# One plan for another: 2239 steps of a fused retention and SwiGLU kernel in a new order

## The chip, the core and the metric

The kernel runs on one core of one Trainium2 chip. The core has five engines that each work through their own instructions in order and wait for one another by semaphores: PE (TensorE, the matmuls, with PEld for its weight loads), DVE (VectorE), ACT (ScalarE), POOL (GpSimd) and SP (SyncE), which here issues nearly all DMA transfers. The metric is the device time of one launch in microseconds (us). Three runs of the kernel before took 639.87, 640.2 and 643.35 us; the median is 640.2 us.

## What is computed

A recurrent retention block (4 batches, 8 heads, 768 positions, head size 64) feeds a SwiGLU feed-forward block (3072 tokens, model size 512, hidden size 1536), all in float32:

```python
gamma = 1.0 - 2.0 ** (-5.0 - np.arange(H, dtype=np.float32))
for t in range(S):
    state = gamma[None, :, None, None] * state + np.einsum('bhd,bhe->bhde', k[:, :, t], v[:, :, t])
    y[:, :, t] = scale * np.einsum('bhd,bhde->bhe', q[:, :, t], state)
...
x = np.ascontiguousarray(attn_out.transpose(0, 2, 1, 3)).reshape(B * S, H * D)
g = x @ w_gate
silu = g * (1.0 / (1.0 + np.exp(-g)))
val = x @ w_val
return (silu * val @ w_out).astype(np.float32)
```

## The kernel before

**Arithmetic.** Every float32 operand of a large product is split into three parts of fewer bits ("near" for weights and hidden values, "far" for tokens), and a product is three groups of matmuls that add up in one PSUM bank. A split is three small steps on a tile: part 0 on ACT, part 1 on DVE, part 2 on DVE or on POOL. So each product of PE waits for pieces of ACT, DVE and POOL.

**Stages.** The 3072 tokens go in four segments, numbered 0 to 3, of 768 tokens each. A segment has its attention, an up stage (gate and value products, 12 units f of the hidden size) and a down stage (12 units f by 6 token blocks). Segment 0's up stage also converts and prepares the weights, and its down stage writes the split down weights to DRAM for the later ones. Segments 1 to 3 compute the up products by seven half-size products of sums (as in Strassen's method). The attention of segment s + 1 runs among the down stage of segment s.

**Order.** All instructions of the kernel belong to named steps. `run()` goes through one string, `PLAN`, and issues each step's instructions when its name comes up; each engine then executes its own in that order. An engine's order is thus what `PLAN` leaves when all other engines' steps are struck out; SP's and ACT's transfers are ordered in the same way. Semaphores are derived from which buffers the steps read and write.

**Names** (`s/` is the segment; segment 0's up stage has none):
- `G f:i`, `W f:i`: gate and value product of unit f in segment 0, 12 matmuls of 384 columns each (L1056); `p`, `v` the same in pieces of 256 columns (L1074). `i f:i` is the silu on ACT (L462), `j f:i` the multiplication on DVE (L462).
- `n f:0` to `n f:5`: the splits of unit f's gate weights (0, 1, 2) and value weights (3, 4, 5) on ACT, DVE and POOL (L1128, L1131, L1134).
- `U` loads raw weights; `a`, `b`, `c` (ACT; L552, L555, L558), `S` (DVE, L565) and `C` (DVE L573 or POOL L575) convert them; `T` makes sums of them on DVE (L417); `Z` stores them.
- `s/p f.n`: the seven products of unit f in segments 1 to 3, six matmuls each (L1229); `s/u f.n` the ten small steps behind them (L1244 to L1248) on ACT and DVE; `s/w f.g.0` to `.2` the splits of group g of unit f's weights (L1128, L1131, and L417 on DVE or L1134 on POOL); `s/L f` their load from DRAM (L1201).
- `s/D f.tok`: three matmuls of 512 columns of the down stage (L1298); `s/h f.k` the splits of the hidden values; `s/W f` the load of the down weights (L1277); `0/d f.0` to `.2` their splits in segment 0 (L1137, L1140, L1144), `0/Z f` their store (L1288); `s/e tok` and `s/o tok` conversion (L1316 to L1329) and store of the output.
- Attention of segment s: `l` loads, `sc` scores, `A`, `B`, `C` the mixing products (all L824), `dec`, `q`, `k` scalings, `was` and `new` the state, `y` copies of results out of PSUM (L1159, L1163 on ACT), `sum` and `x` sums and splits of the tokens, `ta` to `tc`, `cv`, `mv`, `cm` copies of masks and states.

A second set, `ELSE`, decides the engine of some steps: a `w f.g.2` or `0/d f.1` named in it runs on DVE, otherwise on POOL; an `e` named in it goes to the other of ACT and DVE. Buffers for splits rotate in the order in which steps ask for them (four for wide tiles, three for narrow ones). The last argument of the table of planned times (`at`) plays no part where `PLAN` names a step, and it names all.

Of the kernel before, what the change touches and what calls it, by code (L numbers as in the profile page):

```python
# [25 lines left out]
L = 3  # L26
# [51 lines left out]
    W8:1 i8:0 n9:3 b10 j7:0 T8:1 n9:1 n9:2 U16:3 S10 a11 n9:4 G9:0
    k4 i8:1 t4 C15 c10 C10 n9:5 W8:0 g5 n10:0 T8:2 T9:0 b11
    c16 n10:1 G9:1 Z15 j8:0 j8:1 n10:2 a16 n10:3 t5 U17:2 b16 W9:0  # L80
    i9:1 T9:1 0/h0.0 T9:2 S11 Z8 W9:1 S16 G10:1 n10:4 i9:0 C16 c11
    C11 n10:5 n11:0 j9:0 Z9 G10:0 n11:3 Z16 i10:1 j9:1 a17 i10:0 W10:1
    P1 n11:4 T11:0 T11:1 1/was0.0 T11:2 n11:1 W10:0 Z11 c17 n11:2 n11:5 b17
    0/h0.1 0/W0 G11:1 0/h1.0 G11:0 j10:0 0/d0.0 h1 0/h0.2 1/sc0 j10:1 i11:0 0/h1.1
    0/W1 S17 0/d1.0 i11:1 0/d0.1 1/l3 C17 T10:0 1/dec0.0 W11:0 0/d1.1 0/d0.2 W11:1
    0/h2.0 j11:0 0/D0.2 j11:1 1/k0.0 1/l4 1/dec0.1 1/q0.0 0/D0.1 1/q0.1 0/D0.4 1/k0.1 1/l5
    0/D0.0 0/h2.1 0/d1.2 0/h1.2 0/h4.0 0/W2 0/Z0 1/A0 1/y0.06 1/new0.0 0/h4.1 1/y0.01 0/D0.5
    0/D0.3 0/d2.0 1/B0 0/D1.1 0/h3.0 1/y0.03 0/D1.5 1/y0.04 0/Z1 1/y0.02 1/y0.07 1/y0.05 T10:1
    1/was0.1 1/y0.15 1/y0.00 1/y0.14 0/d2.1 0/D1.4 1/y0.12 0/d2.2 0/D1.2 1/y0.13 0/W3 Z17 0/D1.3
    0/Z2 0/d3.0 0/D1.0 0/h2.2 0/h3.1 1/C0 0/W4 T10:2 0/h3.2 0/d3.1 0/h4.2 Z10 1/y0.16  # L90
    1/l7 1/y0.17 1/new0.1 1/sum0.0 0/D2.3 0/D2.1 1/y0.10 0/h5.0 1/begin 1/sum0.1 0/d3.2 0/h5.1 1/y0.11
# [6 lines left out]
    0/D5.5 1/C1 0/d7.0 1/y1.16 0/d7.1 0/D6.5 0/D5.0 1/y1.17 1/y1.15 1/new1.1 0/h7.2 1/y1.14 1/y1.11
    0/D5.1 1/y1.13 1/x1.2.0 0/D6.3 0/d7.2 0/D6.4 0/Z6 1/y1.10 0/D7.3 0/h9.0 1/sc2 0/h8.2 1/x1.2.2
    0/D6.2 1/q2.1 1/k2.1 0/D7.5 0/W8 1/sum1.0 0/D6.1 1/sum1.2 1/k2.0 0/D6.0 0/D7.1 1/x1.1.0 0/h10.0  # L100
    0/h9.1 0/d8.0 0/D7.2 1/dec2.0 1/l10 1/sum1.1 1/dec2.1 0/W9 1/x1.1.1 0/D7.0 0/d8.1 1/x1.2.1 0/Z7
    1/sum1.3 1/was2.0 1/q2.0 1/x1.0.0 1/x1.1.2 0/d9.0 0/D7.4 0/d8.2 0/h11.0 1/A2 1/new2.0 0/D8.0 1/x1.0.1
# [36 lines left out]
    1/h3.0 1/D1.4 2/q0.1 2/B0 2/y0.10 1/D1.2 2/y0.11 1/h5.0 1/h2.2 1/h3.1 1/h3.2 1/h4.1 2/sum0.2
# [1355 lines left out]
```

## Time and profile before

| | us |
|---|---|
| three runs | 639.87, 640.2, 643.35 |
| median | 640.2 |
| the profiled execution, its own time | 641.82 |
| span of its instructions | 639.9 |

The profile is one execution. Busy times are those of its span of 639.9 us; what lies between the span and the execution's own time is launch and end. The page's first lines give each engine's busy time; the chain of waits follows the work that ended last back through what released it; the wait lists tell who waited for whom; groups put equal instructions together (line, engine, operation, tile written and read, shape, count, busy us, mean ns); windows give busy times by stretch. By time, segment 0's up stage lies up to some 132 us, the down stages at about 132 to 197, 286 to 348, 437 to 502 and 588 to 636 us, and the up stages of segments 1 to 3 between them. DMA engines are the busiest in the first stretches: 0.93 of their time from 35 to 127 us.

### The profile page before, as it was taken

What the parts mean: (1) busy time and instruction counts of PE and PEld (TensorE: products, weight loads), DVE (VectorE), ACT (ScalarE), POOL (GpSimd) and SP (SyncE); (2) the same over time, 40 slices, a digit from 0 to 9 for tenths busy, and PEclk for the clock granted to TensorE, in tenths of its full rate; (3) what the DMA queues carried; (4) which work ended last, traced back from release to release, by engine and by line L of the source; (5) the groups of instructions that cost most, each with busy time, mean ns of one, the idle gap of its engine ahead of it and who ended that gap; (6) DMA issues with size and microseconds to landing.
All of it is one profiled execution on the core that took longest, in us unless ns stands there. A gap on an engine that the chain in (4) does not pass through costs nothing.

```text
span 639.9 us, 14128 instructions
## 1 busy us (share of the span) xinstructions
PE 632.4 (99%) x5587; PEld 582.4 (91%) x5587; DVE 502.3 (78%) x759; ACT 397.2 (62%) x845; POOL 181.8 (28%) x121
## 2 busy tenths in 40 slices
PE   8999999999999999999999999999999999999997
PEld 7999999988779999998888999998888999999886
DVE  3998787899898886877698777887887868877641
ACT  3796798777866557656775567666774556555121
POOL 1444445544423255410002343320000155251000
PEclk9999999999999999999999999999999999999999
DMA  9899998789788545588974335565894433514664
GB/s 319 276 347 332 366 319 277 276 319 304 257 283 304 181 148 188 144 249 218 295 239 182 129 125 188 198 189 192 240 376 168 166 115 116 178 32 145 214 197 149
DMA packets 57747, 143.03 MB, mean 224 GB/s; under 512 B 5840, under 2 KB 28368, under 8 KB 57680
## 3 DMA queue, kind: packets, MB, share of 16 engines
q1 hardware_dynamic: 57104, 141.33, 66.1%
q8 instruction: 44, 0.72, 0.5%
q10 hardware_dynamic: 576, 0.79, 0.3%
q14 instruction: 23, 0.19, 0.1%
HBM read 112.21 MB, written 29.88 MB: 222 GB/s over the span
## 4 chain that ended last, share of the span: by engine, by line
PE 92%; DMA 3%; ACT 3%; issue 1%; DVE 1%; SPq 0%; ACTq 0%
PE bank L1229 40%; PE bank L1298 28%; PE bank L1056 13%; PE bank L824 5%; PE bank L1074 3%; DMA hT<-in_k_n_dram 2%; PE bank L650 1%; DMA hT<-in_k_t_dram 1%; ACT states L915 1%; PE bank L741 1%; PE bank L727 1%; PE bank L712 1%; ACT hT L857 1%; ACT local L870 0%; PE bank L691 0%
## 5 line engine op out<-in xcount | busy, mean ns | idle before, releaser
L1298 PE MATMUL bank<-oitem,gitem 128*128 128x512 f32 x867 | 205.2, 393 | 0.0
L1298 PEld LDWEIGHTS bank<-oitem,gitem 128*128 128x128 f32 x867 | 160.3, 188 | 34.5 <-DVE tmp L955 0.4
L1229 PE MATMUL bank<-xa,gitem 128*128 128x384 f32 x864 | 159.6, 335 | 0.2 <-ACT tmp L1244 0.2
L1229 PEld LDWEIGHTS bank<-xa,gitem 128*128 128x128 f32 x864 | 150.5, 188 | 0.9 <-ACT tmp L1244 0.5
L1134 POOL TENSOR_TENSOR gitem<-gitem 128x768 fp32r<-128x768 f32 x42 | 81.6, 1948 | 149.1 <-DVE gitem L1131 128.4
L1134 POOL TENSOR_TENSOR oitem<-oitem 128x512 fp32r<-128x512 f32 (+1 forms) x46 | 52.7, 1148 | 188.8 <-DVE oitem L1131 151.8
L1056 PE MATMUL bank<-xa,oitem 128*128 128x384 f32 x480 | 84.2, 335 | 0.0
L1229 PE MATMUL bank<-xb,gitem 128*128 128x384 f32 x432 | 83.5, 334 | 0.0
L1056 PEld LDWEIGHTS bank<-xa,oitem 128*128 128x128 f32 x480 | 83.0, 188 | 0.2
L1131 DVE SCALAR_TENSOR_TENSOR gitem<-gitem,loads 128x768 fp32r<-128x768 f32 x72 | 74.6, 1048 | 7.7 <-ACT gitem L1128 6.2
L417 DVE SCALAR_TENSOR_TENSOR gitem<-gitem 128x768 fp32r<-128x768 f32 x78 | 77.5, 1002 | 2.2 <-DVE gitem L1131 0.5
L1229 PEld LDWEIGHTS bank<-xb,gitem 128*128 128x128 f32 x432 | 75.8, 188 | 0.2
L1128 ACT ACTIVATE gitem<-loads 128x768 fp32r<-128x768 f32 x72 | 59.3, 844 | 23.2 <-PE bank L1229 18.7
L1128 ACT ACTIVATE gitem<-hT 128x768 fp32r<-128x768 f32 x48 | 39.8, 841 | 39.9 <-PE bank L1298 31.2
L1131 DVE SCALAR_TENSOR_TENSOR gitem<-gitem,hT 128x768 fp32r<-128x768 f32 x48 | 46.2, 962 | 22.3 <-ACT gitem L1128 22.1
L1229 PE MATMUL bank<-xb,oitem 128*128 128x384 f32 x216 | 43.2, 335 | 0.0
L1229 PEld LDWEIGHTS bank<-xb,oitem 128*128 128x128 f32 x216 | 38.0, 188 | 0.1
L1246 ACT COPY tmp<-bank 128x384 f32<-128x384 f32 x36 | 17.3, 481 | 25.0 <-PE bank L1229 22.6
L1246 DVE TENSOR_TENSOR hT<-bank,tmp 128x384 f32<-128x384 f32 x36 | 20.0, 554 | 16.0 <-PE bank L1229 15.2
L1245 ACT COPY tmp<-bank 128x384 f32<-128x384 f32 x36 | 17.3, 480 | 23.0 <-PE bank L1229 17.2
L1244 ACT COPY tmp<-bank 128x384 f32<-128x384 f32 x36 | 17.2, 478 | 21.3 <-PE bank L1229 14.2
L1247 DVE TENSOR_TENSOR hT<-bank,tmp 128x384 f32<-128x384 f32 x36 | 19.9, 552 | 10.6 <-PE bank L1229 10.5
(152 smaller groups left out, 812.5 us busy)
## 6 DMA issues: line engine op xcount, KB each, us to landing
loads<-wup SPq DMA_DIRECT2D x36, 896.0 KB, 5.2
oitem<-wdnt SPq DMA_DIRECT2D x33, 768.0 KB, 4.8
wdnt<-oitem SPq DMA_DIRECT2D x12, 768.0 KB, 5.3
wup<-first SPq DMA_DIRECT2D x9, 896.0 KB, 6.7
rawp<-in_w_gate_dram SPq DMA_DIRECT2D x12, 512.0 KB, 7.1
rawp<-in_w_val_dram SPq DMA_DIRECT2D x12, 512.0 KB, 6.4
rawp<-in_w_out_dram SPq DMA_DIRECT2D x12, 512.0 KB, 5.8
out_dram<-chunk_x SPq DMA_DIRECT2D x21, 256.0 KB, 4.4
```

The lines of the kernel that those rows point to most:

```text
L417: stt(o, x, 1.0, y, op0=mul, op1=op)
L824: nc.tensor.matmul(o, a, b, start=start, stop=True, skip_group_check=True)
L1056: nc.tensor.matmul(o, w[:, a, ts(b, P)], X0[:, a, i, NC - 1 - b], start=a == b == 0, stop=a == 2 and b == NC - 1, skip_group_check=True)
L1074: nc.tensor.matmul(o, w[:, a, ts(b, P)], X0[:, a, :, NC - 1 - b, ts(j, P)], start=a == b == 0, stop=a == 2 and b == NC - 1, skip_group_che ...
L1128: act(o[0], x, AF.Copy, scale=CUT / FAR)
L1131: stt(o[1], f32(o[0]), -FAR, x, op0=mul, op1=add)
L1134: op(o[2], f32(o[0]), f32(o[1]), op=add)
L1229: nc.tensor.matmul(o, w[:, a, k], x[:, a, KH - 1 - k], start=start and a == k == 0, stop=a == 2 and k == KH - 1, skip_group_check=True)
L1245: lambda: act(gate, c11, AF.Silu, scale=ONE), lambda: copy(u2, x),
L1246: lambda: copy(p5, wb), lambda: tt(h1, x, p5, op=add),
L1247: lambda: tt(h0, wb, u2, op=add), lambda: tt(h0, h0, gate, op=mul),
L1298: nc.tensor.matmul(banks[tok][:, cols], hs[f][:, a, ds(i * TH + u * P, P)], wo[f][:, a, cols], start=f == a == 0, stop=f == NF - 1 and a = ...
```

## The change

The first 130 names of `PLAN` stay. The 2239 names behind them are the same names in another order, the loads and stores among them. The order in which buffers are asked for is the same in both, so each step keeps its buffers. `ELSE` keeps its 53 entries in number, but 36 of them are others. Nothing else is edited. Of the order of each engine's steps, 423 of PE's 646 follow another step than before, 608 of DVE's 731, 536 of ACT's 664, 64 of POOL's 117 and 142 of SP's 228.

The diff, cut to the lines that the prediction speaks of (in the plan a line holds a dozen names or more):

```diff
-    G5:0 j4:1 S7 C13 j4:0 G5:1 n6:2 a8 n6:3 P2 n6:4 i5:1 c14
-    W5:1 i5:0 Z13 c7 j5:1 T6:0 n6:5 W5:0 a14 U9:1 U15:0 C7 T5:1
...
-    0/e2 0/o2 1/x2.2.1 1/w0.1.1 1/p1.1 1/x2.2.2 2/ta 1/u0.3 1/w1.1.0 1/u1.0 1/p1.2 1/w0.2.1 1/w0.2.2
...
+    i2:0 T2:0 S4 n3:0 c4 n3:3 i2:1 a5 U13:1 U6:3 T2:1 T2:2 Z2
+    C12 Z12 U7:0 j2:0 C4 n3:1 n3:2 G3:1 n3:4 n3:5 j2:1 G3:0 W3:1
...
+    W4:1 i4:1 j4:1 c6 C6 U14:3 a7 b7 j4:0 n6:0 S7 n5:4 g5
+    n5:2 c7 C7 G5:0 i5:0 T5:0 T5:1 n6:1 C13 Z13 U9:1 T5:2 Z5
+    G5:1 i5:1 a8 n6:3 n5:5 W5:1 j5:1 n6:4 b8 h0 c14 W5:0 j5:0
...
-    "0/e1", "0/e3", "0/e4", "0/e5", "1/e2", "1/e3", "1/e5",
+    "0/d10.1", "0/d11.1", "0/d3.1", "0/d4.1", "0/d6.1", "0/d8.1", "0/d9.1",
```

The other places, told as the order of names:

```
before  1/B0 0/D1.1 ... 0/D1.5 ... 0/D1.4 ... 0/D1.2 ... 0/D1.3 ... 0/D1.0 ... 1/C0
after   1/B0 1/y0.05 1/y0.13 1/y0.02 1/y0.14 1/y0.07 1/y0.15 1/y0.04 1/y0.00 1/y0.12 0/D2.5 0/D2.0 0/D2.4 1/y0.03 1/was0.1 1/C0
before  1/B2 ... 0/D8.5 ... 0/D9.3 ... 0/D9.5 ... 0/D9.4 ... 1/C2
after   1/B2 1/y2.01 1/y2.03 1/x1.2.1 1/y2.06 1/y2.07 0/h10.2 1/y2.05 0/D8.5 0/D8.2 ... 1/y2.02 1/y2.04 1/C2
before  0/D11.5 1/p0.0 ... 1/p1.1 1/x2.2.2 2/ta 1/u0.3 1/w1.1.0 1/u1.0 1/p1.2
after   0/D8.3 0/D8.1 0/D8.4 2/ta ... 1/p1.1 1/w0.1.2 0/e2 0/e3 0/e1 1/u0.3 1/w1.2.0 1/u1.0 1/u1.1 1/p1.2
before  2/l13 2/k2.2 1/D6.5 2/y1.10 2/k2.1 2/y1.11 2/x1.2.0 2/new1.1 2/sc2
after   2/y1.11 2/was1.11 1/D6.3 2/l11 2/l13 2/k2.3 ... 1/D7.3 1/D7.5 1/D7.2 1/h9.0 2/y1.10 ... 2/new1.1 2/sc2 ... 2/k2.2
```

More of the change, by code (lines that the diff above doesn't have):

```diff
@@ L78 @@
[L78 to L91, printed above, removed]
@@ L98 @@
[L98 to L102, printed above, removed]
@@ new lines @@
+    W8:1 T8:2 n10:0 j8:1 n10:1 j8:0 U11:1 Z7 G9:1 C15 Z15 P1 a16
+    k5 t5 b16 G9:0 i9:0 n9:5 W9:0 n10:2 G10:0 Z8 U17:2 S16 C16
+    Z16 P2 a11 b11 S11 T9:0 T9:1 i9:1 n10:3 n10:4 c11 C11 T9:2
+    Z9 W9:1 j9:1 j9:0 h2 n11:0 G10:1 n11:3 n11:4 T11:0 T11:1 T11:2 Z11
+    n11:1 i10:0 0/h0.0 n10:5 W10:1 W10:0 0/W0 i10:1 n11:2 G11:1 T10:0 j10:1 a17
+    b17 c17 1/was0.0 h1 0/h1.0 n11:5 0/h0.1 0/h0.2 S17 C17 G11:0 0/W1 0/d0.0
+    0/d0.1 0/h2.0 0/h4.0 i11:1 0/d1.0 0/d1.1 i11:0 1/l3 1/k0.0 1/sc0 1/l5 1/l4 W11:1
@@ new lines @@
+    j10:0 W11:0 0/W2 0/h1.1 1/dec0.0 T10:1 0/d0.2 0/Z0 0/D0.1 j11:1 j11:0 1/q0.0 1/dec0.1
+    0/D0.0 0/h1.2 0/D0.3 0/D0.2 0/D0.4 0/D0.5 0/d1.2 0/D1.1 T10:2 0/h2.1 1/q0.1 1/k0.1 1/A0
+    1/new0.0 Z17 0/Z1 0/h2.2 0/d2.0 0/d2.1 0/d2.2 0/h3.0 0/h3.1 1/y0.06 0/h4.1 0/h4.2 1/y0.01
+    0/W3 0/Z2 0/D1.3 0/D1.0 0/D1.2 0/D1.5 0/D1.4 0/W4 0/h5.0 0/h5.1 0/h3.2 0/h5.2 Z10
+    1/B0 1/y0.05 1/y0.13 1/y0.02 1/y0.14 1/y0.07 1/y0.15 1/y0.04 1/y0.00 1/y0.12 0/D2.5 0/D2.0 0/D2.4
+    1/y0.03 1/was0.1 1/C0 1/new0.1 1/l7 0/D2.3 0/D2.2 0/D2.1 0/d3.0 1/l6 1/y0.10 1/y0.16 1/y0.11
@@ new lines @@
+    1/w0.1.0 0/D10.3 0/D11.3 1/sum2.3 1/x2.0.0 0/e0 1/x2.2.1 1/w0.0.2 1/p0.0 0/D11.2 1/p0.1 1/x2.2.2 1/x2.0.2
+    1/x2.0.1 0/D11.4 0/D11.5 1/L1 1/w1.0.0 1/w1.0.1 0/Z9 1/w0.2.0 1/u0.0 2/R 0/Z10 1/p0.2 1/u0.1
+    1/w1.0.2 1/p1.0 1/w0.2.1 1/w0.1.1 1/p1.1 1/w0.1.2 0/e2 0/e3 0/e1 1/u0.3 1/w1.2.0 1/u1.0 1/u1.1
+    1/p1.2 0/Z11 1/u0.2 1/w1.1.0 1/w1.1.1 1/w1.2.1 1/p0.3 1/w0.2.2 1/p0.4 1/u0.4 1/p0.5 1/u0.5 1/u0.6
+    1/p0.6 1/L2 1/w2.1.0 1/w2.0.0 1/w2.0.1 1/w2.0.2 1/w2.2.0 1/u1.3 0/o0 1/w1.1.2 1/p1.3 1/u1.4 1/w2.2.1
@@ new lines @@
+    1/D1.3 2/begin 1/h2.2 2/q1.1 2/l8 1/W2 2/k1.3 2/q1.0 2/sum0.2 2/tc 2/l7 1/D1.1 1/D1.4
+    1/D2.5 1/D2.0 1/D2.2 1/D2.4 1/D2.3 1/D2.1 1/W3 1/W4 1/W5 1/h3.1 1/h3.2 1/D3.3 1/D3.5
+    1/D3.2 1/D3.4 2/l14 1/h4.1 2/k1.1 2/y0.11 2/sum0.0 2/sum0.1 1/h5.0 2/x0.1.0 2/x0.1.2 2/x0.1.1 1/h5.1
+    2/k1.0 2/k1.2 2/was0.11 1/D3.1 2/sum0.3 1/h5.2 1/h4.2 1/D4.2 2/x0.2.0 2/was0.10 2/new0.1 2/x0.2.1 2/x0.0.0
+    1/D3.0 1/D4.1 1/D4.0 1/D4.5 2/mv0.1 2/was1.00 1/h6.0 2/was1.01 2/x0.2.2 2/A1 1/D4.3 2/y1.00 2/y1.01
@@ new lines @@
+    1/h6.1 2/new1.0 2/mv1.0 1/D5.3 1/W6 1/D5.2 2/x0.0.2 1/h6.2 1/D5.5 1/D4.4 1/h7.0 1/h8.0 1/h7.1
+    1/D5.4 1/h7.2 2/x0.0.1 1/D5.1 2/B1 2/y1.11 2/was1.11 1/D6.3 2/l11 2/l13 2/k2.3 1/D5.0 1/D6.0
+    1/W7 1/D6.1 1/D6.5 1/D6.4 2/l12 1/W8 1/D6.2 1/W9 2/L0 2/q2.0 1/D7.3 1/D7.5 1/D7.2
+    1/h9.0 2/y1.10 2/was1.10 2/x1.2.0 1/h8.1 2/q2.1 1/h8.2 2/sum1.0 2/new1.1 2/sc2 2/was2.01 2/x1.1.0 2/k2.1
+    2/sum1.1 2/sum1.3 2/x1.2.2 1/h9.1 2/x1.1.1 2/dec2.0 2/x1.1.2 2/sum1.2 2/dec2.1 1/h10.0 2/k2.0 2/x1.0.0 2/mv1.1
@@ new lines @@
+    3/x1.1.0 2/h6.0 3/x1.2.0 3/new1.1 3/x0.0.2 2/D4.2 2/D4.3 2/D4.5 2/D4.0 2/h6.1 3/x1.1.2 2/h7.0 2/h7.1
+    2/h6.2 2/W5 2/W6 3/l13 3/k2.3 3/k2.0 2/D5.2 3/x1.1.1 3/sum1.0 3/mv1.1 3/k2.1 3/k2.2 3/was2.00
+    2/D5.3 2/D5.4 3/sc2 3/dec2.1 2/D5.1 2/D5.0 2/D6.1 2/D5.5 2/D6.3 2/D6.5 2/D6.4 2/D6.2 2/D6.0
+    3/q2.0 3/x1.2.1 3/sum1.2 3/sum1.1 2/h7.2 3/dec2.0 2/W7 2/D7.3 3/l12 2/D7.2 2/h8.0 2/h8.1 2/h9.0
+    3/x1.2.2 2/h8.2 2/h10.0 3/sum1.3 3/x1.0.0 3/was2.01 2/D7.1 2/D7.0 3/A2 2/D7.4 2/h9.1 3/new2.0 3/x1.0.2
```

298 lines of the change are left out of this document (141 added, 157 removed).

## The prediction

> **What bounds the kernel now.** I read the page's first lines, then the chain of waits in order of time, then PE's own waits and the short timelines around them, then groups and windows by stage.
>
> ```profile
> span 639.9 us, 14128 instructions
> PE 632.4 (99%) x5587; PEld 582.4 (91%) x5587; DVE 502.3 (78%) x759; ACT 397.2 (62%) x845; POOL 181.8 (28%) x121
> PEclk9999999999999999999999999999999999999999
> ```
> ```profile
> 46.73 58.25 PE bank L1056 x336
> ...
> 348.42 77.05 PE bank L1229 x444
> ...
> 501.76 84.30 PE bank L1229 x486
> ...
> 587.82 48.47 PE bank L1298 x216
> 636.31 0.43 DVE chunk_x L1321
> ```
>
> PE is 99% busy at an undiminished clock. A busy PE could still be a slow one, so I divide: 336 matmuls in 58.25 us are 0.173 us each, 444 in 77.05 and 486 in 84.30 the same, over stretches that lie 450 us apart. So the 384-column matmuls run at one pace everywhere, and the 512-column ones at 48.47 / 216 = 0.224 us. PE's own wait list says how little is left.
>
> ```profile
> PE bank L1413 <- DVE warm L1428: 1.1, 1, 1.1
> PE bank L650 <- DMA hT<-in_k_t_dram: 1.0, 1, 1.0
> PE bank L824 <- issue: 0.6, 1, 0.6
> PE bank L650 <- DVE tmp L656: 0.4, 1, 0.4
> PE bank L712 <- DVE hT L671: 0.4, 1, 0.4
> PE bank L1229 <- ACT tmp L1244: 0.2, 1, 0.2
> ```
> ```profile
> 201.17 0.86 PE L1229 MATMUL bank<-xb,gitem 128*128 128x384 f32 x4
> ...
> 202.25 0.62 PE L1229 MATMUL bank<-xa,gitem 128*128 128x384 f32 x2 [0.22 <-ACT tmp L1244]
> ```
> ```profile
> 320.27 0.26 PEld L824 LDWEIGHTS bank<-loads 64*64 64x64 f32 x11 [0.27 <-DVE states L923]
> ```
> ```profile
> 309.04 9.13 DMA hT<-in_k_n_dram
> ```
>
> The L1413, L650 and L712 waits, 2.9 us, belong to the warm-up and the first chunks, whose steps stand within the first 130 and stay. Behind them two rows remain: 0.6 at "issue", for which the profile shows no other work, and 0.2 at L1229. That 0.2 counts from a modelled end; by starts, four matmuls from 201.17 at 0.173 would let the next begin at 201.86, and it began at 202.25: 0.39 us. The weight loads show one more stop, 0.27 at L824. So **what a new order can win back is 0.39 + 0.27 = 0.7 us**, with the issue gap 1.3. The kernel is bound by PE's work, and the change leaves that work as it is.
>
> **The change part by part.** Compared name by name, the two plans hold the same 2369 steps; no matmul, buffer or transfer is added or removed. PE goes from an attention step (L824) to a wide one 28 times in either order, so what such a change costs is paid as often. Removed work: nothing. What can change is who is late when PE arrives.
>
> *Waits that go.* At 202 us the first silu copy of the unit (1/u0.3, then 1/u1.0) stood on ACT behind 2/ta, three mask copies; the new plan puts 2/ta among the 0/D8 steps. The 0.27 came from the copy 2/y1.11, which stood on ACT behind 2/k2.2, and that behind the transfer 2/l13 (the row of 9.13 us); the new plan has 2/y1.11 ahead of 2/l13 and 2/k2.2 behind 2/sc2. I count both as gone: **−0.7**.
>
> *Waits that come.* I read the new plan for places where a chain on DVE, ACT and POOL has less PE work beside it than its own length.
>
> ```profile
> L1134 POOL TENSOR_TENSOR oitem<-oitem 128x512 fp32r<-128x512 f32 x21 | 28.6, 1362 | 40.7 <-DVE oitem L1131 36.3 <-PE bank L1056 4.3
> L1131 DVE SCALAR_TENSOR_TENSOR oitem<-oitem,first 128x512 fp32r<-128x512 f32 x15 | 11.4, 762 | 1.3 <-ACT oitem L1128 1.3
> L462 DVE TENSOR_TENSOR hT<-bank,tmp 128x384 f32<-128x384 f32 x18 | 9.7, 548 | 2.4 <-PE bank L1056 2.4
> L573 DVE CUSTOM_DVE_ANT_0 first<-bank,first 128x2048 uint16<-128x2048 uint16 x7 | 8.5, 1221 | 1.8 <-ACT first L558 1.7
> L565 DVE SCALAR_TENSOR_TENSOR bank<-first,bank 128x1024 uint32<-128x1024 uint32 x6 | 7.4, 1226 | 3.6 <-ACT bank L555 3.6
> L555 ACT ACTIVATE bank<-first 128x1024 int32<-128x1024 f32 x6 | 6.2, 1032 | 0.1
> ```
> ```profile
> L1298 PE MATMUL bank<-oitem,gitem 128*128 128x512 f32 x216 | 52.7, 397 | 0.0
> ...
> L1163 ACT COPY chunk_x<-bank 64x128 f32<-64x128 f32 x48 | 12.4, 260 | 10.1 <-PE bank L824 7.2 <-issue 1.1 <-DVE states L1031 1.0
> ```
>
> (Groups of the stretches 35 to 127 us and 127 to 197 us; count, busy us, mean ns.)
>
> - G3:1. A product is 12 matmuls, 12 × 0.173 = 2.08 us; its last third, which reads the weights' third part, begins after 1.39. The new plan has W2:0, W2:1, then G3:1. After W2:0, DVE does j2:0 (0.55), C4 (1.22) and n3:1 (0.76), then POOL n3:2 (1.36): 3.89 us against PE's 2.08 + 1.39 = 3.47. **+0.4.** Before, n3:2 stood ahead of W2:0, three products from its use.
> - W5:1. After W4:1: j4:1 0.55, C6 1.22, b7 1.03, S7 1.23, n5:4 0.76, n5:5 1.36, together 6.15, against G5:0, G5:1 and two thirds of W5:1, 5.55. **+0.6.** Before, n5:5 stood ahead of G5:0.
> - 1/C0 overwrites banks that ten ACT copies of 1/y0 read after 1/B0: 2.6 us. Between stand three 0/D steps, nine matmuls at 0.224, 2.0 us; before there were six. **+0.5.**
> - 1/C2: seven copies, 1.8 us, against two 0/D steps, 1.35 us; before there were four. **+0.4.**
>
> Together 1.9. From below each is nothing, if the chain has begun earlier than I assume; from above the first two grow by half a POOL piece in DVE's or POOL's way (1.36 / 2 = 0.7) and the others by one more ACT piece (0.3), so 1.9 + 2.0 = 3.9. I take 1.9, which is made of means of this very stage.
>
> *Engines exchanged.* The set ELSE changes too. 29 of the w steps' sums go from DVE to POOL and 26 from POOL to DVE; seven 0/d steps go from POOL to DVE; ten stores' conversions swap between ACT and DVE, a net four to DVE.
>
> ```profile
> L1134 POOL TENSOR_TENSOR gitem<-gitem 128x768 fp32r<-128x768 f32 x42 | 81.6, 1948 | 149.1 <-DVE gitem L1131 128.4
> L417 DVE SCALAR_TENSOR_TENSOR gitem<-gitem 128x768 fp32r<-128x768 f32 x78 | 77.5, 1002 | 2.2 <-DVE gitem L1131 0.5
> ```
> ```profile
> 127.00:197.00 70.00, 69.95 (x982) 56.46 (x981) 64.74 (x91) 50.67 (x140) 27.13 (x17) 1.00 0.86 297
> ...
> 502.00:588.00 86.00, 86.00 (x496) 85.82 (x495) 69.55 (x107) 49.11 (x95) 31.66 (x20) 1.00 0.36 122
> ```
> ```profile
> L1144 DVE SCALAR_TENSOR_TENSOR oitem<-oitem 128x512 fp32r<-128x512 f32 x12 | 10.3, 859 | 0.1
> ...
> L417 DVE SCALAR_TENSOR_TENSOR loads<-loads,tab 128x512 f32<-128x512 f32 x3 | 2.0, 679 | 0.0
> ...
> L1144 DVE SCALAR_TENSOR_TENSOR xb<-chunk_x,xb 128x512 fp32r<-128x512 f32 x3 | 2.0, 679 | 0.0
> ```
>
> (Windows list length, then busy us of PE, PEld, DVE, ACT and POOL.) A w sum takes 0.95 us longer on POOL (1.95 against 1.00). In the up stages POOL is busy 31.66 of 86 us and DVE 69.55, so both have room: priced at 0, at worst one product late by 0.95. The 0/d steps are the delicate ones. Seven at 0.68 (the same shape, L417) put 4.8 us on a DVE that is idle for 70 − 64.74 = 5.3 us there. I price them at 0 because idle time still covers them and POOL's pieces leave; without that cover they cost up to 4.8.
>
> The same shape takes 679 ns in one L1144 row and 859 in another, in the stage where POOL works beside DVE. [...]
>
> *Loads moved.* 142 of 228 transfer steps follow another one on SP's queue than before.
>
> ```profile
> loads<-wup SPq DMA_DIRECT2D x36, 896.0 KB, 5.2
> oitem<-wdnt SPq DMA_DIRECT2D x33, 768.0 KB, 4.8
> ```
> ```profile
> 186.42 0.32 SPq L1201 DMA_DIRECT2D loads<-wup  x1
> 190.79 0.80 SPq L1288 DMA_DIRECT2D wdnt<-oitem  x2
> ```
> ```profile
> 196.80 1.08 PE bank L1229 x6
> ```
>
> SP waits in order, so a load that waits for its buffer holds all behind it. Read by place, the down weights come earlier: 1/W3, 1/W4 and 1/W5 now stand together ahead of the 1/D3 steps, where 1/W4 stood directly ahead of 1/D4.2. The clearest that comes later is 1/L2, from ahead of the stores 0/Z10 and 0/Z11 to behind them: by these rows from 186.42 to 190.79 + 0.80 = 191.6, and it lands 5.2 later, at 196.8. Its first reader, 1/w2.1.0 on ACT, stands behind 1/p0.6, the seventh product after 196.80, so not before 196.80 + 7 × 6 × 0.173 = 204.1. Priced at 0, with 7.3 us of cover; from above one landing, 5.2; from below nothing, since no PE wait behind the start names a transfer.
>
> **Sum.** −0.7 + 1.9 = +1.2 us on the profiled execution's 641.8 (span 639.9): 643.0. The runs' median was 640.2; the same +1.2 on it is **641.4**. The forecast is no change that can be told.
>
> **Rivals.**
> - *DVE becomes the bound between 127 and 197 us* (slower). For it: 5.3 us idle against 4.8 added, and 0/d.1, 0/d.2, 0/D follow each other closely. [...] It decides once usable idle time falls below the added work. Price half to all of 4.8: 643.8 to 646.2, say 645. Chance 0.20. This is also the way in which the change is not just an order.
> - *A load comes late* (slower): one of the 142 loses its cover because something ahead of it on SP's queue waits, and a landing shows: all of it gives 641.4 + 5.2 = 646.6, half of it 644. Against it: 1/L2's 7.3 us. Chance 0.09. [...]
> - *No new wait*: the four chains start early enough: 640.2 − 0.7 = 639.5, with the issue gap gone 638.9. Chance 0.14; also no change.
> - *Faster*: 637.0 or less needs 3.2 us where waits offer 1.3, so PE's pace itself would have to rise: the 216 wide matmuls of 127 to 197 us are busy 52.7 us against 48.47 at the end, 4.2 us lost around attention. About 637 or a little below. But the number of such changes is equal. Chance 0.07.
>
> **How the numbers follow.** The forecast has 0.50. A measurement of this kernel tells about 0.5%, 3.2 us (637.0 to 643.4). Same: 0.50 + 0.14 = 0.64; slower: 0.20 + 0.09 = 0.29; faster 0.07. Predicted time 641.4. Its own range goes from 639.5 (no new wait) to 643.4 (1.9 grown to 3.9). With the rivals I reach down to 638.0, which leaves the faster case out, and up to 646.5, where nearly all of DVE's 4.8 is paid.
>
> **What would show it.** PE's wait list should again hold well under 4 us behind the start, with short waits at L1056 near 56 and 78 us behind POOL L1134 and at L824 near 146 and 183 us behind ACT L1163; none at 1/p1.2. POOL's L1140 count should fall from 12 to 5 and DVE's busy time in 127 to 197 us stay below 70. The prediction is wrong if PE waits for a transfer, if 0/D steps wait for L1144, or if the matmuls' pace differs from 0.173 and 0.224.

## The result, and the profile after

| | before | after |
|---|---|---|
| median, first comparison (9 runs each) | 641.37 us | 644.66 us |
| ratio, 95% interval | | 1.006 (1.0037 to 1.0083) |
| median, second comparison (23 and 12 runs) | 642.72 us | 644.5 us |
| ratio, 95% interval | | 1.0032 (1.002 to 1.0044) |
| profiled execution, its own time | 641.82 us | 644.26 us |
| span | 639.9 us | 642.5 us |

The changed kernel takes 0.3 to 0.6% longer, some 2 to 3 us. Both intervals lie above 1, so the loss is small but clear of noise. The forecast was 641.4 with a range from 638.0 to 646.5: the result lies inside it, though the loss is larger than the +1.2 us of the sum.

The page of after, its first lines and the granted clock, and below them two rows of its chain of waits (start, length, work, count of instructions):

```profile
span 642.5 us, 14114 instructions
PE 631.6 (98%) x5587; PEld 580.2 (90%) x5587; DVE 508.1 (79%) x767; ACT 393.5 (61%) x841; POOL 177.1 (28%) x117
PEclk9999999999999999999999999999999999999999
```
```profile
349.91 77.04 PE bank L1229 x444
...
591.06 47.69 PE bank L1298 x213
```

The pace is what it was: 77.04 / 444 = 0.173 us, 47.69 / 213 = 0.224. The matmuls are the same, so the added time is in waits. PE's wait list of after (us in total, times, longest):

```profile
PE bank L650 <- DMA hT<-in_k_t_dram: 1.9, 2, 1.5
PE bank L824 <- issue: 1.5, 1, 1.5
PE bank L1056 <- POOL oitem L1134: 1.2, 2, 0.7
PE bank L1413 <- DVE warm L1428: 1.1, 1, 1.1
PE bank L824 <- ACT chunk_x L1163: 0.4, 1, 0.4
PE bank L741 <- DMA hT<-in_v_n_dram: 0.4, 1, 0.4
PE bank L650 <- DVE tmp L656: 0.4, 1, 0.4
PE bank L1298 <- DMA oitem<-wdnt: 0.2, 1, 0.2
```

Compared with before, L1056 behind POOL and L824 behind ACT are new, a down weight comes late once, "issue" has grown from 0.6 to 1.5, and L1229 behind ACT L1244 is gone. This list counts from modelled ends, so I size waits by starts: how much later than its pace the next matmul began. In segment 0 that gives 0.87 at 56.17 us (G3:1), 0.66 at 78.15 and 0.13 at 76.69 (W5:1), 0.58 at 147.86 (1/C0), 0.32 and 0.17 at 185.2 and 185.5 (1/C2): 2.7 together, at the four places that the forecast named. Put in order of time, by matmul starts:

| stretch of PE's work | before | after | what differs |
|---|---|---|---|
| start to the first product of 384 columns | 46.56 | 45.58 | -0.98: first transfers, steps not touched |
| from there to the last product of segment 1 | 239.25 | 241.93 | +2.68: the four places +2.71, 1/p1.2 -0.39, others +0.36 |
| from there to the last matmul | 350.19 | 350.94 | +0.75: issue in 3/B0 +0.92, 1/D1.2 for its load +0.40, 2/sc2 -0.35, others -0.22 |

The first stretch differs by chance: over the kernels below (all but pe_shift), which share its steps, it took from 45.9 to 46.8 us. So from the first product on, after is 3.4 us behind in this execution.

### The profile page after: what moved, and what is told of

Its sections match the earlier page's. It is cut to its first block, busy times and chain, and to the rows that moved or that the text cites. A ratio compares the mean times of both kernels' runs of the same rounds, so it can differ in the third digit from the quotient of the medians.

```text
span 642.5 us, 14114 instructions
## 1 busy us (share of the span) xinstructions
PE 631.6 (98%) x5587; PEld 580.2 (90%) x5587; DVE 508.1 (79%) x767; ACT 393.5 (61%) x841; POOL 177.1 (28%) x117
## 4 chain that ended last, share of the span: by engine, by line
PE 91%; DMA 4%; ACT 2%; DVE 1%; issue 1%; POOL 0%; SPq 0%; ACTq 0%; POOLq 0%
PE bank L1229 38%; PE bank L1298 31%; PE bank L1056 11%; PE bank L824 6%; PE bank L1074 3%; DMA oitem<-wdnt 1%; DMA loads<-in_k_t_dram 1%; DMA hT<-in_q_t_dram 1%; DMA hT<-in_k_t_dram 1%; PE bank L650 1%; PE bank L727 1%; PE bank L741 1%; ACT chunk_x L1163 1%; PE bank L712 0%; POOL oitem L1134 0%
## 5 line engine op out<-in xcount | busy, mean ns | idle before, releaser
L1229 PE MATMUL bank<-xa,gitem 128*128 128x384 f32 x864 | 160.8, 335 | 0.0
L1229 PEld LDWEIGHTS bank<-xa,gitem 128*128 128x128 f32 x864 | 150.7, 188 | 1.0 <-ACT tmp L1246 0.4
L1134 POOL TENSOR_TENSOR gitem<-gitem 128x768 fp32r<-128x768 f32 x43 | 84.9, 1982 | 179.0 <-DVE gitem L1131 165.2
L1134 POOL TENSOR_TENSOR oitem<-oitem 128x512 fp32r<-128x512 f32 (+1 forms) x48 | 55.3, 1158 | 170.7 <-DVE oitem L1131 131.6
L1056 PE MATMUL bank<-xa,oitem 128*128 128x384 f32 x480 | 85.2, 336 | 1.2 <-POOL oitem L1134 1.2
L1056 PEld LDWEIGHTS bank<-xa,oitem 128*128 128x128 f32 x480 | 82.9, 188 | 2.5 <-POOL oitem L1134 2.1
L1229 PE MATMUL bank<-xb,gitem 128*128 128x384 f32 x432 | 83.8, 335 | 0.0
L1229 PEld LDWEIGHTS bank<-xb,gitem 128*128 128x128 f32 x432 | 75.7, 188 | 0.5 <-DVE gitem L417 0.2
L417 DVE SCALAR_TENSOR_TENSOR gitem<-gitem 128x768 fp32r<-128x768 f32 x77 | 74.7, 979 | 1.2
L1131 DVE SCALAR_TENSOR_TENSOR gitem<-gitem,hT 128x768 fp32r<-128x768 f32 x48 | 49.1, 1031 | 18.5 <-ACT gitem L1128 18.4
L1229 PE MATMUL bank<-xb,oitem 128*128 128x384 f32 x216 | 43.4, 335 | 0.0
L1229 PEld LDWEIGHTS bank<-xb,oitem 128*128 128x128 f32 x216 | 38.0, 188 | 0.0
L1244 ACT COPY tmp<-bank 128x384 f32<-128x384 f32 x36 | 17.2, 479 | 18.3 <-PE bank L1229 14.7
```

Source lines behind the costliest of these rows:

```text
L417: stt(o, x, 1.0, y, op0=mul, op1=op)
L1056: nc.tensor.matmul(o, w[:, a, ts(b, P)], X0[:, a, i, NC - 1 - b], start=a == b == 0, stop=a == 2 and b == NC - 1, skip_group_check=True)
L1131: stt(o[1], f32(o[0]), -FAR, x, op0=mul, op1=add)
L1134: op(o[2], f32(o[0]), f32(o[1]), op=add)
L1229: nc.tensor.matmul(o, w[:, a, k], x[:, a, KH - 1 - k], start=start and a == k == 0, stop=a == 2 and k == KH - 1, skip_group_check=True)
L1244: steps = (lambda: copy(p1, x), lambda: tt(c11, z, p1, op=add), lambda: act(gate, c11, AF.Silu, scale=ONE), lambda: copy(u2, x), lambda: c ...
```

## The experiments

The theory was that the four late chains make most of the new time. The rivals were DVE as the bound between 127 and 197 us, and the growth of the "issue" gap. "First part" below is the second stretch of the table, 239.25 us before and 241.93 after; it repeats well (242.00 in the second execution of after).

### up_early: the up stage's two chains undone

```diff
-    i2:0 T2:0 S4 n3:0 c4 ... C4 n3:1 n3:2 G3:1
+    i2:0 T2:0 S4 n3:0 n3:1 n3:2 c4 ... C4 G3:1
-    n5:3 n4:5 W4:0 ... S7 n5:4 g5 ... n6:3 n5:5 W5:1
+    n5:3 n4:5 n5:4 n5:5 W4:0 ... S7 g5 ... n6:3 W5:1
```

> The order of after, with four names moved back: n3:1 and n3:2 directly behind n3:0, n5:4 and n5:5 directly behind n4:5. Theory (the new time is made of late chains): the waits at L1056 behind POOL L1134 near 56 and 78 us (0.87 and 0.66 us by matmul starts) are gone, a short one of 0.1 to 0.3 may show at another product, the two at L824 behind ACT L1163 stay, and segment 0's up stage ends 1.3 to 1.6 us earlier than in after, all of which reaches the end: about 643.0 by the median of after (644.7). Rival (the lost time is DVE's load in 127 to 197 us or another pace): the two waits go, but what they gave comes back as waits between 127 and 197 us, and the end does not move: 644 to 645.

Measured: 643.31 us, ratio to before 1.002 (1.0004 to 1.0037). The first part took 240.59 us, 1.34 less than in after. The waits of 0.87 and 0.79 are gone; in their place stand 0.30 at G5:0 (POOL L1134) and 0.31 at W6:0 (DVE's L462). The gain stayed, so these chains did cost what the trace shows, and the rival that gives it back in the down stage falls. Of the 1.65 us, 0.6 came back as shorter waits a few products later. The gain is read from the first part, which repeats; the medians alone do not show it, since the interval of up_early meets both intervals of after.

### all_early: the down stage's two chains as well

```diff
-    1/y0.03 1/was0.1 1/C0 1/new0.1 1/l7 0/D2.3
+    1/y0.03 1/was0.1 0/D2.3 1/C0 1/new0.1 1/l7
-    1/y2.04 1/C2 ... 1/y2.16 0/D9.5
+    1/y2.04 0/D9.5 1/C2 ... 1/y2.16
```

> As the kernel before it, and 0/D2.3 ahead of 1/C0 and 0/D9.5 ahead of 1/C2, so that one more down step (0.67 us) stands between the copies and the products that overwrite their banks. Theory: all four late chains are covered, the waits at L824 behind ACT L1163 (0.58 near 146 us, 0.49 near 183 us by matmul starts) fall to under 0.15 together, and the kernel ends 2.3 to 2.7 us ahead of after: about 642, within 0.3% of before, what is left against before being a load of 0.4 and the issue gap of 0.9. Rival (DVE is the bound in 127 to 197 us): the waits at L824 go, and waits of the 0/D steps for L1144 or L1163 at later places take as much, so no gain over the kernel with only the up stage mended.

Measured: 643.64 us, 1.0017 (1.0004 to 1.0031): no gain over up_early, against an expected gain of about 1. The first part took 241.22, even 0.63 more than in up_early. Weight loads of all_early in order of time (start, length, what, idle time ahead and what ended it):

```profile
185.48 0.19 PEld L1298 LDWEIGHTS bank<-oitem,gitem 128*128 128x128 f32 x1 [0.54 <-DVE oitem L1144]
...
190.48 3.31 PEld L1298 LDWEIGHTS bank<-oitem,gitem 128*128 128x128 f32 x15 [0.45 <-DVE oitem L1144]
194.32 1.70 PEld L1298 LDWEIGHTS bank<-oitem,gitem 128*128 128x128 f32 x8 [0.54 <-DVE oitem L1144]
```

The waits at 1/C0 and 1/C2 are gone, and three waits for the third split part of the down weights (L1144) stand in their place; near 150.5 us the next attention step now has the shorter cover, waits 0.2 for L1163 and takes 0.4 longer. So those two waits are in the trace of after, but not what the kernel loses by: behind them DVE and ACT are late by as much. Here the rival named the right next engine.

### d_on_dve: before, with only the seven 0/d steps moved to DVE

```diff
+    "0/d10.1", "0/d11.1", "0/d3.1", "0/d4.1", "0/d6.1", "0/d8.1", "0/d9.1",
```

> The kernel before, in its own order, with the seven steps 0/d3.1, 0/d4.1, 0/d6.1, 0/d8.1, 0/d9.1, 0/d10.1 and 0/d11.1 on DVE and not on POOL. Theory: nothing, -0.3 to +0.5 us on before, since DVE gets seven pieces of 0.68 us (4.8) but loses most of its waiting beside POOL's pieces, so its busy time in 127 to 197 us rises by under 2 us from 64.7, and no wait of a 0/D step for L1144 of more than 0.3 appears. Rival (DVE becomes the bound there): busy time rises by 4 to 5 us to 69 or more, 0/D steps wait for L1144, and the kernel takes 2.4 to 4.8 us longer than before.

Measured: 642.97 us, 1.0014 (0.9999 to 1.0028). The windows list for 127 to 197 us (length, then busy us of PE, PEld, DVE, ACT, POOL), and the third split's group there, of d_on_dve:

```profile
127.00:197.00 70.00, 69.60 (x980) 56.23 (x980) 64.96 (x98) 50.66 (x140) 16.93 (x11) 1.00 0.84 294
```
```profile
L417 DVE SCALAR_TENSOR_TENSOR gitem<-gitem 128x768 fp32r<-128x768 f32 x12 | 11.9, 995 | 0.1
L1144 DVE SCALAR_TENSOR_TENSOR oitem<-oitem 128x512 fp32r<-128x512 f32 x12 | 9.9, 821 | 0.2 <-POOL oitem L1140 0.2
L417 DVE SCALAR_TENSOR_TENSOR oitem<-oitem 128x512 fp32r<-128x512 f32 x7 | 4.8, 690 | 1.8 <-ACT oitem L1137 1.8
```

DVE has seven instructions more (x98 for x91), 4.8 us of them, and is busy 64.96 us where it was 64.74. Nearly all of the 4.8 came back from its other pieces, as POOL's busy time there fell from 27.13 to 16.93. No down step waits for L1144; a wait of 0.43 us for L1163 at 147.66 is new, and the "issue" gap near 444 us came out at 1.29 with PE's order untouched (0.82 in before). So the seven steps do not make DVE the bound in before's order.

### else_alone and order_alone: one half of the change each

else_alone is before's plan with after's set `ELSE`; order_alone is after's plan with before's set.

> The order of before with the set ELSE of after: 29 w sums on POOL that were on DVE, 26 on DVE that were on POOL, the seven 0/d steps on DVE, four e conversions net on DVE. By the prediction's pricing (both engines have room, 0 each, one product late by 0.95 at worst): 0 to +1.0 us on before. Rival (the set and the order belong together): where the order leaves a w sum just the 1.00 us of DVE before its product, the 1.95 us of POOL, and its wait for a part 1 on DVE, make the product late each time, in the up stages of segments 1 to 3 at 5 to 10 places with 1 to 4 us each: 650 to 665 us, and PE's wait list names POOL L1134 at L1229.

> The order of after with the set ELSE of before, the counterpart of else_alone (682.0). Theory (an order is made for its set): the w sums that this order leaves little time are on POOL again, so it also costs 20 to 40 us on before: 660 to 685, with waits at L1229 behind POOL L1134 and DVE L417. Rival (the order of after is the weaker of the two, its set does no harm): 640 to 646.

Measured: 682.01 and 684.06 us, ratios 1.0622 (1.0589 to 1.0654) and 1.0641 (1.0612 to 1.0669), each from two runs. For else_alone that is more than either expectation, for order_alone it is the upper end of what was expected. PE's wait list of else_alone, and then two of its windows (the third figure from the end is the clock that PE was granted):

```profile
PE bank L1229 <- DVE gitem L417: 12.1, 7, 3.0
PE bank L1229 <- POOL gitem L1134: 6.4, 2, 5.3
PE bank L1229 <- DVE oitem L417: 3.2, 1, 3.2
PE bank L1229 <- DVE chunk_x L1327: 2.0, 1, 2.0
```
```profile
583.00:588.00 5.00, 0.33 (x1) 0.33 (x2) 2.96 (x3) 0.00 (x0) 4.68 (x3) 0.69 0.56 184
588.00:592.00 4.00, 4.00 (x14) 4.00 (x14) 0.66 (x2) 2.02 (x4) 1.39 (x1) 0.54 0.00 0
```

The waits come at w sums (L417 on DVE, L1134 on POOL), up to 5.3 us at once, 21.7 in the first three rows; the last row is a store's conversion. In order_alone the same two lead the list, L417 with 9.0 us and L1134 with 7.2. In and behind the longest wait of else_alone the granted clock fell to 0.69 and 0.54. The rows leave 16 us of the added 39.5 (span 679.4 against 639.9), and much of that is matmuls at a lower clock: the mean over the run is 0.98, and 0.02 of 679.4 is 14 us, an estimate. The price of 0 for the exchange of engines holds only with the order that comes with it, and for the order likewise.

### pe_shift: every instruction of PE some places later

```diff
     warm_up(8)
+    for _ in range(20):
+        nc.tensor.matmul(banks[3][:, :16], warm[:, :P], warm[:, :16], start=True, stop=True,
+                         skip_group_check=True)
```

> After, with 20 small matmuls (128x128 by 16 columns of zeros, into the bank that the warm-up writes) behind the warm-up's eight, within the time in which PE waits for the first transfer. They move every later instruction of PE 20 matmuls on in its instruction stream and change no order. Theory of the gap in 3/B0: it stands at a place of PE's instruction stream (weight load 4219 of before, 4220 of after), not at a step, so it now comes 20 matmuls earlier in the program, ahead of 3/B0 among the 2/D steps, where matmuls of 0.22 us leave room for it: the gap of 1.6 us in 3/B0 is gone and the end comes 0.7 to 1.5 us earlier than in after, if the start is no later. Rival: the gap belongs to 3/B0 (a release that the profile does not name): it stays inside 3/B0 with 1 us or more, and the time is that of after or up to 0.5 us more.

Measured: 653.25 us, 1.0178 (1.0152 to 1.0204). The time tells nothing, since the small matmuls ran as 40 and took 8.55 us, longer than the wait that they were to fill. The gap tells more. PE's timeline of pe_shift:

```profile
4.66 8.55 PE L1432 MATMUL bank<-warm 128*128 128x16 f32 x40
...
347.65 0.33 PE L824 MATMUL bank<-hT 64*64 64x64 f32 x3 [0.85 <-issue]
...
449.81 0.34 PE L824 MATMUL bank<-loads,chunk_x 64*64 64x64 f32 x10
449.94 0.90 PE L824 MATMUL bank<-chunk_x,loads 64*64 64x64 f32 x47
453.93 0.71 PE L824 MATMUL bank<-chunk_x,loads 64*64 64x64 f32 x17 [3.09 <-issue]
```

It has left 3/B0 for the attention steps ahead of it. Counted in matmuls from the start of those, it stands behind 143, in after behind 183: just the 40 that were added. (The expectation's 4219 and 4220 are not the trace's count: 4167 weight loads stand ahead of the gap in before, 4166 in after.) So the gap belongs to a place in PE's instruction stream, as expected; that it would hide among the down steps was wrong, since it landed in attention and is larger there.

The place can be named. I count PE's records up to the gap: matmuls, their weight loads and those of PE's sequencer. In before, after, up_early, all_early, d_on_dve, b0_close, after_again and pe_shift alike the gap stands behind 8384 of them. pe_shift has a second stop at "issue" that after does not have, 1.06 us by starts at 347.65, behind 6848. A short stop in before's order, 0.26 us at 182.69 (at "issue" with 0.35 in d_on_dve and 0.44 in b0_close), stands behind 3777. These are 192, 192 and 193 past a multiple of 256, and 256 of PE's records to a packet is what the 44 packets of the instruction queue come to, as the page of after shows below.

### b0_apart and b0_close: down steps ahead of 3/B0

```diff
b0_apart (on up_early)
-    2/D0.3 2/W1 2/D1.1 3/B0 3/l9 2/W2 2/D0.2 2/D1.2
+    2/D0.3 2/W1 2/D1.1 2/D0.2 2/D1.2 3/B0 3/l9 2/W2
b0_close (on before)
-    2/W1 2/D1.0 3/y0.01 3/mv0.0 3/B0
+    2/W1 3/y0.01 3/mv0.0 3/B0 2/D1.0
```

> The order of up_early with two more down steps, 2/D0.2 and 2/D1.2, moved ahead of 3/B0, so that six of them and not four stand behind 3/A0. Theory (instruction fetch): PE's instructions come in blocks of 16 KiB (44 packets of queue q8 in the profile, 256 instructions each); 3/sc1, 3/A0 and 3/B0 use up one block in less time than the next needs to arrive, so each down step of 0.67 us put between them shortens the gap at issue in 3/B0 by as much: two steps by 1.3 us, from 1.6 to 2.4 (after, up_early, all_early) to 0.3 to 1.1, and the end comes about 1.3 us earlier than in up_early: 642.0 by its median of 643.3. Rival (the gap belongs to a place in the stream and takes its time there, whatever stands around): it moves by six matmuls within 3/B0 and stays at 1.5 or more; no gain.

> The kernel before with one edit: the down step 2/D1.0 is moved from ahead of 3/B0 to behind it, so that four of them and not five stand between 3/A0 and 3/B0, as in after. Theory (instruction fetch): the gap at issue in 3/B0 grows by the step's 0.67 us, from 0.8 to about 1.5 as in after, and the kernel takes 0 to 0.7 us longer than before; nothing else changes. Rival (the gap's size is chance, or comes of the rest of after's order): the gap stays at 0.8.

The expectations count 2/D0.0 and 2/D0.1 among the steps between, though they stand ahead of 3/A0; the differences of one and two steps are right. Measured: b0_apart 642.4 us, 1.0002 (0.9989 to 1.0015), where up_early had 1.002 (on another chip, and with a late down weight of 0.56 us in its trace that b0_apart's has not); b0_close 642.7, 1.0011 (0.9998 to 1.0025), not to be told from before. So with the two up chains and the gap taken out, the new order is level with the old one. PE's timelines of before, after and b0_apart at 3/B0:

```profile
441.01 2.35 PE L1298 MATMUL bank<-oitem,gitem 128*128 128x512 f32 x9
443.29 0.45 PE L824 MATMUL bank<-tab,loads 64*64 64x64 f32 x15
444.34 0.47 PE L824 MATMUL bank<-tab,loads 64*64 64x64 f32 x17 [0.60 <-issue]
```
```profile
442.51 1.65 PE L1298 MATMUL bank<-oitem,gitem 128*128 128x512 f32 x6
444.09 0.50 PE L824 MATMUL bank<-tab,loads 64*64 64x64 f32 x17
446.11 0.40 PE L824 MATMUL bank<-tab,loads 64*64 64x64 f32 x12 [1.52 <-issue]
```
```profile
442.74 2.21 PE L1298 MATMUL bank<-oitem,gitem 128*128 128x512 f32 x9
444.88 1.00 PE L824 MATMUL bank<-tab,loads 64*64 64x64 f32 x30
```

Ahead of 3/B0 stand 9, 6 and (three of them in the row before) 12 matmuls of 512 columns; after has one down step fewer than before. The DMA records of the trace hold the other half. A row of after's page, third part (queue, packets, MB, share):

```profile
q8 instruction: 44, 0.72, 0.5%
```

All 44 packets have 16,384 bytes. PE's records, 5587 matmuls, 5587 weight loads and 83 of its sequencer, are 11,257 (76 and 11,250 in before, which also has 44 packets); at 256 to a packet either makes 44. So I read q8 as PE's instructions. For the packet that 3/B0 needs (times from the start of 3/A0, the gap from start to start):

| kernel | down steps between | 3/B0 begins | packet begins | has landed | PE goes on | gap |
|---|---|---|---|---|---|---|
| before | 3 | 4.77 | 2.92 | 4.30 | 5.82 | 0.82 |
| after | 2 | 4.09 | 3.31 | 4.54 | 6.11 | 1.74 |
| after_again | 2 | 4.12 | 4.87 | 6.02 | 7.39 | 2.99 |
| up_early | 2 | 4.10 | 4.19 | 5.50 | 6.84 | 2.46 |
| all_early | 2 | 4.11 | 3.43 | 4.69 | 6.02 | 1.63 |
| b0_close | 2 | 4.07 | 3.06 | 4.18 | 5.42 | 1.00 |
| b0_apart | 4 | 5.45 | 3.13 | 4.40 | 5.95 | 0.27 |
| d_on_dve | 3 | 4.77 | 3.65 | 4.87 | 6.30 | 1.29 |
| else_alone | 3 | 4.77 | 2.81 | 4.10 | 5.33 | 0.32 |
| order_alone | 2 | 4.11 | 3.82 | 5.15 | 6.67 | 2.27 |
| before_mended | 4 | 5.45 | 3.25 | 4.42 | no stop | none |
| before_mended, again | 4 | 5.45 | 3.06 | 4.45 | no stop | none |

In every row with a stop PE goes on 1.2 to 1.6 us behind the landing, whether 3/B0 began early or late, and with four steps between there is next to nothing left to wait for. So the place in the stream says where PE can run out of instructions, and the long matmuls ahead of it say how much of the fetch they cover. The rows give 1.0 to 3.0 us with two steps between, 0.3 to 1.3 with three, at most 0.3 with four. The landing itself varies from 4.10 to 6.02 between executions, more than two down steps (1.35 us), so one execution of each can't show what one step is worth: b0_close came out at 1.00 and not at 1.5 because PE went on 0.4 us earlier than in before. (The profiled execution of b0_close also waited 1.5 us for a late down weight.)

### before_mended (twice) and after_again

before_mended is before with 2/ta ahead of 0/e0, 2/y1.11 ahead of 2/l13, and 2/D1.2 ahead of 3/B0.

> The kernel before with three edits: 2/ta ahead of 0/e0, 2/y1.11 ahead of 2/l13, and 2/D1.2 ahead of 3/B0. The first two are the prediction's waits that go, alone, without the rest of the new order: the waits before 1/p1.2 (0.39 us by starts) and 2/sc2 (0.27 to 0.35) should be gone and nothing come for them, -0.7. The third is one more down step for the fetch of the instructions: the gap at issue falls from 0.8 to 0.1 to 0.3, -0.6. Together 1.3 us less than before, ratio 0.998. Rival (a wait that goes off PE only hands the time to the next late one): less than 0.5 us, not to be told from before.

> The kernel before_mended once more, beside after_again on one chip. Theory: its three edits are worth 1.3 us on before, ratio 0.998 (0.9991 with an interval of 0.9972 to 1.001 in its first runs), and 0.6 to 0.8% on after. Rival: no difference to before, ratio 0.999 to 1.001.

> The changed kernel as it is, for the ratio on the chip of these runs. From its trace: late chains 2.7 us, issue gap 0.7 to 1.5 more than before, less 0.7 for the two waits gone and up to 1.4 either way by the first transfers: ratio 1.004 to 1.006, the gap at issue in 3/B0 again 1.5 to 2.5 us, the waits at L1056 behind L1134 again 0.8 to 0.9 and 0.6 to 0.7 by matmul starts.

Measured: before_mended 641.14 us, 0.9991 (0.9972 to 1.001), and again 641.01, 0.9978 (0.9961 to 0.9996); after_again 644.5, 1.0032, a little under the expected ratio, with the waits at L1056 at 0.87 and 0.65 by starts, as expected, and the gap at issue at 2.99, above the expected 1.5 to 2.5. Both first parts of before_mended took 238.37, 0.88 less than before: 0.50 at 1/p1.2 (0.39, and 0.11 at the matmul behind it) and 0.26 at the stop at 182.69, which no edit touches. At 2/sc2 the edit did less than expected: 0.22 of the 0.35 is left, again behind DVE's L923. The issue gap in 3/B0 is gone. In the last stretch a new wait of 0.3 (a 2/D step for L417 near 454 us) and late down weights, 1.2 us in the second execution, took most of what was gained there. It is the fastest of all kernels here, ahead of before by 0.1 to 0.2% and of after by 0.5%, though only the second interval leaves 1 out.

## Why the prediction was nearly right

**What bounds the kernel: right.** PE's pace stayed, and from before to after the time moved with PE's waits. **Waits that go: right in after.** Nothing stops at 1/p1.2 or 2/sc2 there. Alone, in before_mended, the edit at 1/p1.2 gives its whole gain and the one at 2/sc2 a third.

**Waits that come: right places, sizes too small.** The terms were 0.4, 0.6, 0.5 and 0.4, measured 0.87, 0.79, 0.58 and 0.49: 2.7 where the sum said 1.9, inside its upper end of 3.9. The last two were right but for the subtraction: 2.6 - 2.02 is 0.58 and 1.82 - 1.34 is 0.48, and the forecast wrote 0.5 and 0.4. The first two were undersized. The largest miss, G3:1, in the timeline of after (PE, DVE, POOL):

```profile
50.26 5.21 PE L1056 MATMUL bank<-xa,oitem 128*128 128x384 f32 x29
56.17 1.14 PE L1056 MATMUL bank<-xa,oitem 128*128 128x384 f32 x5 [0.70 <-POOL oitem L1134]
...
52.09 0.56 DVE L462 TENSOR_TENSOR hT<-bank,tmp 128x384 f32<-128x384 f32 x1 [0.56 <-PE bank L1056]
52.56 1.22 DVE L573 CUSTOM_DVE_ANT_0 first<-bank,first 128x2048 uint16<-128x2048 uint16 x1
53.70 1.28 DVE L1131 SCALAR_TENSOR_TENSOR oitem<-oitem,loads 128x512 fp32r<-128x512 f32 x2
...
54.55 2.82 POOL L1134 TENSOR_TENSOR oitem<-oitem 128x512 fp32r<-128x512 f32 x2 [3.77 <-DVE oitem L1131]
```

PE would have gone on at 56.17 - 0.87 = 55.30 and, 20 matmuls of 0.173 earlier, began W2:1 at 51.84; DVE's first piece starts 0.25 later, a handover that I left out. From there to 56.17 the chain takes 4.08 us, where the sum of means was 3.89. Piece by piece, DVE's three end at 54.38, after 2.29 us where their means add up to 2.53; POOL starts 0.17 later, a second handover; its first piece ends at 56.12 and took 1.57, not 1.36; PE goes on 0.05 behind it. At W5:1 the start is 0.25 late too (71.71 to 71.96), and the chain takes 6.19 against 6.15. The term that failed is thus the chain's length: mean durations alone, without the handovers between engines. At G3:1 these are 0.47 in sum, and the pieces' differences from their means nearly cancel.

What such a wait is worth is a second matter, and there the forecast had nothing: the two of the up stage were worth 1.34 of 1.65 when taken away, the two of the down stage nothing, as DVE's L1144 and ACT's L1163 were just as late behind them.

**Engines exchanged: right as a sum, wrong as a step.** Here the rows of after, which have the order too:

```profile
127.00:197.00 70.00, 69.45 (x981) 56.12 (x979) 65.66 (x98) 51.15 (x146) 16.39 (x10) 1.00 0.85 294
```
```profile
L1144 DVE SCALAR_TENSOR_TENSOR oitem<-oitem 128x512 fp32r<-128x512 f32 x12 | 8.3, 688 | 1.6 <-POOL oitem L1140 1.4
L1140 POOL TENSOR_TENSOR oitem<-oitem 128x512 fp32r<-128x512 f32 x5 | 7.9, 1584 | 15.6 <-ACT oitem L1137 8.7 <-DMA tmp<-in_k_n_dram 6.8
```

The signs came as named: L1140 counts 5, DVE is busy 65.66, below 70. In d_on_dve DVE's other pieces gave back 4.6 of the 4.8, and the L1144 row of 859 ns was only one of several that shrank (to 821 there): the 256-column L417 on `tmp` went from 565 to 417 ns as well. No run shows the half of 4.8 at which the rival's price begins: the seven steps added 0.2 us to DVE's busy time. But "both engines have room, so 0" was no reason for the w sums: with the same room in before's order, the set cost some 40 us, nearly all at w sums, while its seven 0/d steps alone cost next to nothing (d_on_dve). So the price of 0 came out right by luck: it holds for this order, and nothing in the forecast looked at that.

**Loads moved: nearly right.** One late load, 0.4 us at 1/D1.2, which by the forecast's own test counts against it. 1/W1 took 8.0 us to land, from 283.70 to 291.67, where the median of its kind is 4.4. It is no fixed cost: after_again, which is the same kernel, shows no such wait in PE's list, nor do all_early and b0_apart with the same loads, while up_early has one of 0.56 at the same step.

**The rivals.** DVE did not become the bound at the price given, but it stands right behind ACT there, as all_early shows; a load came late in small; new waits did come, and the pace did not rise.

**What was missing.** The issue gap in 3/B0 was taken for a fixed 0.6 for which the profile shows no other work. By the table of packets PE goes on 1.2 to 1.6 us behind a landing, so I read it as a wait for instructions; its length depends on how many down steps stand between 3/A0 and 3/B0 (1.0 to 3.0 us with two, 0.3 to 1.3 with three), and the new plan put one fewer there (0.68 us earlier). In the traces that is 0.9 us; with 0.8 from the undersized chains and 0.4 from the late load it brings the forecast's +1.2 to 3.3, where the trace has 3.4 from the first product on and the medians 2 to 3. The issue gap of after also varies by more than 1 us from one execution to the next (1.74 and 2.99), so no single figure for it is safe.

## What to carry to other kernels

A chain's length is its pieces plus a handover at each change of engine (0.03 to 0.25 us in the two chains here); a late chain is priced by what is late behind it, not by its own wait. An order and its assignment of engines are one thing: neither half can be priced alone from mean durations. Where PE goes through tiny matmuls (here 183 of 64x64, with as many weight loads) with few long ones among them, put long ones between: the gap at 3/B0 was 1.0 to 3.0 us with two down steps there and at most 0.3 with four.

## What the runs showed of the hardware

- q8 moved 44 packets of 16,384 bytes, which I read as PE's instructions (11,257 records in after, 256 to a packet). PE stood still for 0.3 to 3.3 us in dense attention steps (160 matmuls of 64x64 and as many weight loads in 2.5 us, then more of them), and in 3/B0 it went on 1.2 to 1.6 us behind the landing of a packet. Every stop at "issue" that PE's wait lists show inside the attention steps, over all traces here, stands 192 or 193 recorded instructions past a multiple of 256.
- The gap can cost twice. In the windows of up_early behind its gap of 2.46 us, the granted clock (third figure from the end) fell:

```profile
444.00:447.00 3.00, 0.75 (x35) 0.67 (x38) 1.78 (x3) 2.26 (x9) 0.00 (x0) 0.98 0.48 138
447.00:449.00 2.00, 2.00 (x73) 1.88 (x67) 0.00 (x0) 0.00 (x0) 0.00 (x0) 0.50 0.64 188
449.00:451.00 2.00, 2.00 (x7) 1.60 (x8) 1.35 (x3) 1.44 (x3) 0.00 (x0) 0.68 0.39 108
```

  Behind the 3.30 us of pe_shift it was 0.55 and 0.50 from 453 to 459 us; in after_again a gap of 2.99 us left it at 1.00. So the clock fell behind gaps of 2.46 and 3.30 us and not behind one of 2.99. The forecast priced no fall of the clock behind a wait; that was too hopeful for the gap at issue. The execution of up_early that the windows show took 646.43 us where its kernel's median is 643.31.
- DVE's pieces lose time beside POOL's, but not evenly. Seven pieces more on DVE and seven fewer on POOL left DVE's busy time nearly as it was (64.74 and 64.96 us). Against the fastest of the same shape, L1144 on `oitem` in before lost 2.2 us of the 3.1 in which POOL worked beside it (127 to 197 us), L417 on `gitem` 1.6 of 3.4, and L955, which reads a PSUM bank, 0.02 of 2.7.
